# Moving a fifth of the integer shifts of an attention kernel into accumulating DMAs, with output weights loaded late and a fused feature map

## Chip, cores, metric

One core of one Trainium2 chip. The metric is the device time of one execution in microseconds (us), the median of several. Engines: PE is TensorE (matmuls; PEld its weight loads), ACT is ScalarE, DVE is VectorE, POOL is GpSimd, SP is the sync engine, which here only issues DMAs.

## The reference, cut to what matters

```python
x = A_x                                             # 2048 x 512, bfloat16
g = sigmoid((x * gate_w).sum(-1, keepdims=True))
# A: softmax attention, 32 heads of 16 columns
p = softmax(einsum("bhqd,bhkd->bhqk", q, k) * 16**-0.5)
a = einsum("bhqk,bhkd->bhqd", p, v)  # ... @ A_wo
# B: linear attention on the same x
phi = lambda t: where(t > 0, t + 1, exp(t)) + 1e-6
b = (phi(q) @ (phi(k).T @ v)) / (phi(q) @ sum(phi(k)))   # ... @ B_wo
return g * a + (1 - g) * b
```

The exponential of 32 x 2048 x 2048 scores is the bulk of the work: 2048 tiles of 128 x 512.

## The kernel before

The kernel shares these tiles between two engines. ACT takes two at a time with its exponential. DVE takes one at a time with a bit trick: it writes score + constant as a 16-bit integer whose bits are a bfloat16 near the exponential ("op1"). To smooth the trick's error, each such tile is used three times, with 0, 43 and 86 added to the integer, and three value matrices with matched factors. The two extra copies are integer additions, the "shifts". They are made for pairs of tiles, on DVE or on POOL:

```python
def d_finish(cur):                      # both tiles of a pair are converted
    # ... cut ...
    for k, m in enumerate(SHIFTS[1:]):  # SHIFTS = (0, 43, 86)
        dst["shifts"].append((cur, m, z, k + 1))

def cand_shift(E=DV):
    # ... cut: take the next shift, find a free Z slot (16 of them) ...
    if E is PO:
        return C(PO, 400, 70 + 484 * n, lambda: nc.gpsimd.tensor_tensor(
            Z[:, z, 0:512 * n].bitcast(I32), Z[:, z0, 0:512 * n].bitcast(I32),
            mcon[:, kt - 1:kt].to_broadcast([128, 256 * n]), ALU.add), ...)
    # ... cut ...
    return C(DV, 450 if hot else 300, 69 + 134 * n, lambda: nc.vector.tensor_scalar(
        Z[:, z, 0:512 * n], Z[:, z0, 0:512 * n], float(m), None, op0=ALU.add), ...)
```

All instructions are ordered when the kernel is built. A list scheduler carries a clock for each engine, books a duration for each candidate (`70 + 484 * n` ns above), and always places what can start first. The program gives every engine its list, with waits on semaphores in it: in the trace of before POOL is idle for 105.1 us ahead of its shifts, 66.1 us of it ended by DVE's tiles. **So a duration booked too short does not give a wrong result; it puts an instruction in front of others that could have run.** That booked clock is called the schedule here, and no trace shows it. The schedule of the kernel before ends at 672.2 us, 18 us below its time.

The feature map phi of branch B was four operations: exponential on ACT, max on DVE, min on POOL, add on POOL:

```python
yield ac(480, ... activation(eb[:, i, :], bank(b), ACT.Exp) ...)
yield dv(607, ... tensor_scalar(mb[:, i, :], bank(b), 0.0, 1e-6, op0=ALU.max, op1=ALU.add) ...)
yield ("FREE", b)
yield po(640, ... tensor_scalar(eb[:, i, :], eb[:, i, :], 1.0, 0.0, op0=ALU.min, op1=ALU.max) ...)
yield po(1300, ... tensor_tensor(dst_ap, eb[:, i, :], mb[:, i, :], ALU.add) ...)
```

The softmax here doesn't subtract the row's maximum and nothing guards it: scores larger than these inputs give would overflow.

## Time and profile before

| | before |
|---|---|
| time, median | 690.25 us (689.38 to 692.46, four runs) |
| exponentials on ACT (two tiles each) | 707 |
| tiles on DVE | 634 |
| shifts on DVE / POOL | 226 / 408 |

The head of the profile page (busy us of each engine, share of the span, instructions; granted TensorE clock in 40 slices, in tenths):

```profile
span 688.1 us, 24195 instructions
PE 676.8 (98%) x9923; PEld 204.2 (30%) x9923; DVE 607.2 (88%) x1084; ACT 669.2 (97%) x746; POOL 536.8 (78%) x600
...
PEclk9999999999999999999999999999999999999999
```

Groups of instructions of before (line, engine, operation, out<-in, shapes, count | busy us, mean ns of one | idle us before them, and what ended it):

```profile
L750 ACT ACTIVATE P<-ps 128x1024 bf16<-128x1024 f32 x707 | 656.8, 1129 | 5.6 <-PE ps L355 5.6
L723 POOL TENSOR_TENSOR Z<-Z,mcon 128x512 int32<-128x512 int32 x408 | 422.9, 1061 | 105.1 <-DVE Z L671 66.1
L671 DVE TENSOR_SCALAR Z<-ps 128x512 int16<-128x512 f32 x634 | 424.6, 682 | 57.8 <-PE ps L355 52.4
L728 DVE TENSOR_SCALAR Z<-Z 128x1024 int16<-128x1024 int16 x226 | 92.2, 437 | 0.6
...
L1027 POOL TENSOR_TENSOR phiK<-eb,mb 128x512 bf16<-128x512 f32 x32 | 41.0, 1282 | 7.3 <-DVE Z L671 3.0
```

The exponentials (L750) are the limit: ACT is busy all the time and idle before them for only 5.6 us in the whole span. PE shows 98% too, but part of that is filler matmuls on the tile `warm` (703 of them, 76.3 us busy), which the scheduler places in PE's gaps; the granted clock was 1.000 in the mean. To get faster, ACT must get fewer tiles, so DVE must take more.

### The profile page before, as it was taken

The numbers are of one execution on the slowest core, as the hardware profiler recorded it, in microseconds if no ns is written. First come the engines' busy times: TensorE is split into PE (matmuls) and PEld (weight loads), VectorE is DVE, ScalarE is ACT, GpSimd is POOL, SyncE is SP. The second block draws the span as 40 slices with busy tenths as digits, with TensorE's granted clock in tenths as the row PEclk, the third lists the DMA queues.
The fourth block names the chain that finished last, engine by engine and source line by source line (L and its number), as shares of the span: only waits on it lengthen the run. The fifth ranks groups of instructions, "written<-read, shape, count | busy, mean of one in ns | idle before, by whom it ended". The sixth has DMA issues, their size and how long they took to land.

```text
span 688.1 us, 24195 instructions
## 1 busy us (share of the span) xinstructions
PE 676.8 (98%) x9923; PEld 204.2 (30%) x9923; DVE 607.2 (88%) x1084; ACT 669.2 (97%) x746; POOL 536.8 (78%) x600
## 2 busy tenths in 40 slices
PE   8899999999999999999999999999999999999998
PEld 3323232222323232222333323232333322222222
DVE  6799989889988898988889888989889899988995
ACT  6899999999999999999999999999999999999995
POOL 3748888887898879886887888878889985588860
PEclk9999999999999999999999999999999999999999
DMA  6920000000000000000000000000011210000001
GB/s 131 301 66 11 6 5 7 2 10 1 5 8 2 9 4 1 10 2 10 2 11 3 4 9 2 10 2 3 17 25 34 49 25 25 17 10 16 18 17 40
DMA packets 27869, 15.97 MB, mean 23 GB/s; under 512 B 19696, under 2 KB 26736, under 8 KB 27760
## 3 DMA queue, kind: packets, MB, share of 16 engines
q1 hardware_dynamic: 26416, 13.91, 7.6%
q8 instruction: 79, 1.29, 0.8%
q10 hardware_dynamic: 1344, 0.52, 0.3%
q14 instruction: 30, 0.25, 0.1%
HBM read 6.69 MB, written 2.10 MB: 13 GB/s over the span
## 4 chain that ended last, share of the span: by engine, by line
PE 67%; ACT 20%; issue 8%; SPq 2%; DVE 1%; DMA 1%; POOL 0%; ACTq 0%; POOLq 0%
PE ps L355 52%; ACT P L750 19%; PE ps L361 15%; SPq L332 2%; ACT eb L1023 1%; DMA xT<-in_A_x_dram 1%; DVE Z L671 0%; POOL Z L723 0%; DVE Zbd L1057 0%; SPq L336 0%; DVE T L988 0%; ACTq L1407 0%; POOL T L1011 0%; ACT wA L1150 0%; POOLq L1407 0%
## 5 line engine op out<-in xcount | busy, mean ns | idle before, releaser
L750 ACT ACTIVATE P<-ps 128x1024 bf16<-128x1024 f32 x707 | 656.8, 1129 | 5.6 <-PE ps L355 5.6
L723 POOL TENSOR_TENSOR Z<-Z,mcon 128x512 int32<-128x512 int32 x408 | 422.9, 1061 | 105.1 <-DVE Z L671 66.1
L671 DVE TENSOR_SCALAR Z<-ps 128x512 int16<-128x512 f32 x634 | 424.6, 682 | 57.8 <-PE ps L355 52.4
L355 PE MATMUL ps<-Qz,KT 32*128 32x512 bf16 x2048 | 276.3, 384 | 2.5 <-ACT P L750 1.2
L355 PE MATMUL ps<-Z,Vc 128*17 128x512 bf16 x1902 | 269.8, 382 | 1.4 <-DVE T L988 1.1
L355 PE MATMUL ps<-P,Vc 128*17 128x512 bf16 x1414 | 246.2, 383 | 0.0
L355 PEld LDWEIGHTS ps<-Qz,KT 32*128 32x128 bf16 x2048 | 68.8, 91 | 263.8 <-ACT P L750 243.7
L728 DVE TENSOR_SCALAR Z<-Z 128x1024 int16<-128x1024 int16 x226 | 92.2, 437 | 0.6
L355 PEld LDWEIGHTS ps<-Z,Vc 128*17 128x17 bf16 x1902 | 61.4, 88 | 71.4 <-issue 42.5
L355 PE MATMUL ps<-warm 128*32 128x512 bf16 (+18 forms) x703 | 76.3, 335 | 1.4 <-POOL warm L408 1.4
L355 PEld LDWEIGHTS ps<-P,Vc 128*17 128x17 bf16 x1414 | 55.8, 88 | 58.3 <-issue 45.8
L1027 POOL TENSOR_TENSOR phiK<-eb,mb 128x512 bf16<-128x512 f32 x32 | 41.0, 1282 | 7.3 <-DVE Z L671 3.0
L361 PE MATMUL ps<-xT,wA 128*32 128x512 bf16 x512 | 43.5, 383 | 0.9 <-DMA xT<-in_A_x_dram 0.6
L355 PEld LDWEIGHTS ps<-warm 128*32 128x32 bf16 (+1 forms) x703 | 23.0, 95 | 20.7 <-issue 14.1
L988 DVE STREAM_TRANSPOSE T<-ps 128x512 f32<-128x512 f32 x32 | 22.8, 712 | 4.7 <-PE ps L355 4.0
L955 POOL TENSOR_SCALAR Vc<-Vc 128x576 bf16<-128x576 bf16 x32 | 21.9, 684 | 5.7 <-DVE Vc L952 2.0
L1026 POOL TENSOR_SCALAR eb<-eb 128x512 f32<-128x512 f32 x32 | 20.0, 625 | 8.0 <-ACT P L750 2.7
L1024 DVE TENSOR_SCALAR mb<-ps 128x512 f32<-128x512 f32 x32 | 21.8, 680 | 2.5 <-ACT eb L1023 1.9
L1011 POOL TENSOR_TENSOR T<-T,rg 128x256 bf16<-128x256 f32 x31 | 19.5, 628 | 5.1 <-DVE Z L728 1.6
L361 PE MATMUL ps<-wA,xT 128*32 128x128 bf16 x1024 | 21.8, 220 | 1.4 <-issue 1.2
L361 PE MATMUL ps<-xT,wB 128*32 128x512 bf16 x256 | 22.9, 383 | 0.0
L1023 ACT ACTIVATE eb<-ps 128x512 f32<-128x512 f32 x32 | 22.8, 714 | 0.0
(80 smaller groups left out, 303.9 us busy)
## 6 DMA issues: line engine op xcount, KB each, us to landing
Qz<-QT SPq DMA_DIRECT2D x120, 16.0 KB, 1.8
wA<-in_A_wqkv_dram SPq DMA_DIRECT2D x1, 1536.0 KB, 7.1
wB<-in_B_wqkv_dram SPq DMA_DIRECT2D x1, 1536.0 KB, 11.7
xnat<-in_A_x_dram SPq DMA_DIRECT2D x3, 512.0 KB, 12.1
out_dram<-outt SPq DMA_DIRECT2D x12, 128.0 KB, 1.7
woA<-in_A_wo_dram SPq DMA_DIRECT2D x1, 512.0 KB, 13.8
woB<-in_B_wo_dram SPq DMA_DIRECT2D x1, 512.0 KB, 9.5
out_dram<-wA SPq DMA_DIRECT2D x4, 128.0 KB, 1.8
```

What stands on the lines that cost most here:

```text
L355: return lambda: nc.tensor.matmul(o, lhsT=l, rhs=r, start=start, stop=stop, skip_group_check=sg)
L361: h = nc.tensor.matmul(o[32 * j:32 * j + 32], lhsT=l[:, 32 * j:32 * j + 32], rhs=r, start=start, stop=stop, skip_group_check=True)
L671: return C(DV, 400, 533 * n + 74, lambda: nc.vector.tensor_scalar(o, i, ZB, 0.0, op0=ALU.add, op1=ALU.max), [r_bank[b] for b in bks], r_Z[ ...
L723: return C(PO, 400, 70 + 484 * n, lambda: nc.gpsimd.tensor_tensor(Z[:, z, 0:512 * n].bitcast(I32), Z[:, z0, 0:512 * n].bitcast(I32), mcon[ ...
L728: return C(DV, 450 if hot else 300, 69 + 134 * n, lambda: nc.vector.tensor_scalar(Z[:, z, 0:512 * n], Z[:, z0, 0:512 * n], float(m), None, ...
L750: return C(AC, 500, 427 * n + 49, lambda: nc.scalar.activation(P[:, slot, 0:512 * n], bank(b0, n), ACT.Exp, scale=ESC), [r_bank[b0 + k] fo ...
L955: yield po(690, lambda k=k: nc.gpsimd.tensor_scalar(Vc[:, k, vs].rearrange("p a b c -> p (a b c)"), Vc[:, 0, vs].rearrange("p a b c -> p ( ...
L988: yield dv(607, lambda: nc.vector.transpose(T1[:, a, :], bank(7)), [r_bank[7]], [r_T1[a]])
L1023: yield ac(480, lambda: nc.scalar.activation(eb[:, i, :], bank(b), ACT.Exp), [r_bank[b]], [r_eb[i]])
L1024: yield dv(607, lambda: nc.vector.tensor_scalar(mb[:, i, :], bank(b), 0.0, 1e-6, op0=ALU.max, op1=ALU.add), [r_bank[b], r_eb[i]], [r_mb[i]])
L1026: yield po(640, lambda: nc.gpsimd.tensor_scalar(eb[:, i, :], eb[:, i, :], 1.0, 0.0, op0=ALU.min, op1=ALU.max), [r_eb[i]], [r_eb[i]])
L1027: yield po(1300, lambda: nc.gpsimd.tensor_tensor(dst_ap, eb[:, i, :], mb[:, i, :], ALU.add), [r_eb[i], r_mb[i]], dst_res)
```

## The change

The intent: relieve DVE and POOL, so that DVE converts more tiles and ACT fewer. A slot `ZD` is preset by plain DMAs with the constants 43 and 86. Then one DMA with an add, issued on POOL, adds the pair of converted tiles to both halves at once: 512 KB written, in place of two shift instructions. The memory comes from the output weights, which now load late over used parts of `wA`, and from fusing the feature map, which drops a POOL add and a buffer. DVE's shifts also yield when an op1 is about to be ready (`HOLD`).

```diff
+    NZD = 2          # slots
+    ZDD = 1000.0     # booked POOL time of an issue, ns
+    ZDL = 4500.0     # booked time to landing, ns
-        woA = SB([128, NCC, D], BF16, "woA")
-        woB = SB([128, NCC, D], BF16, "woB")
+        woA = wA[:, :, D:2 * D]
+        woB = wA[:, :, 2 * D:3 * D]
+        ZD = SB([128, NZD, NTERM - 1, 512 * NB], I16, "ZD")
+        mrow = SB([128, NTERM - 1, 256], I16, "mrow")
... (the loads of woA and woB move from the start to a task that runs at 23/32 of the rounds)
+        def cand_zfill():                                   # two presets a slot, on SP
...
+                for k in range(NTERM - 1):
+                    fin = dma(SP, ZD[:, i, k, :].rearrange("p (a b) -> p a b", b=256),
+                              mrow[:, k, :].unsqueeze(1).to_broadcast([128, 2 * NB, 256]), semZP[i], ...)
+        def cand_dshift():                                  # one accumulating DMA a pair, on POOL
...
+                fin = dma(PO, ZD[:, i, :, 0:512 * n], Z[:, z, 0:512 * n].unsqueeze(1).to_broadcast([128, NTERM - 1, 512 * n]),
+                          semZA[i], zd_add[i], ZDL, [*r_Z[z][0:n]], [r_ZD[i]], name=f"dshift{i}", issue=ZDD, accum=True)
...
+            if E is DV and dst["op1"]:                      # a shift yields to an op1 that is nearly ready
...
+                if wait < HOLD:
+                    return None
... (phi)
-            yield dv(607, ... mb = max(bank, 0) + 1e-6 ...)
-            yield ("FREE", b)
-            yield po(640, ... eb = min(eb, 1) ...)
-            yield po(1300, ... dst = eb + mb ...)
+            yield po(640, ... eb = min(eb, 1 + 1e-6) ...)
+            yield dv(607, lambda: nc.vector.scalar_tensor_tensor(dst_ap, bank(b), 1e-6, eb[:, i, :], op0=ALU.max, op1=ALU.add), ...)
+            yield ("FREE", b)
```

More of the change, by code (lines that the diff above doesn't have):

```diff
@@ L168, in bass_gated_mix__mha_block__linear_attn_block__prompt_kernel @@
     STICK = 0.0
+    HOLD = 100.0
     NB = 2
@@ L172, in bass_gated_mix__mha_block__linear_attn_block__prompt_kernel @@
     NPS, NZ, NQZ, NVQ = 10, 16, 3, 6
+    NZD = 2
+    ZDD = 1000.0
+    ZDL = 4500.0
+    ZDK = 24
     with ExitStack() as es:
@@ L217, in bass_gated_mix__mha_block__linear_attn_block__prompt_kernel @@
         eb = SB([128, 2, 512], FP32, "eb")
-        mb = SB([128, 2, 512], FP32, "mb")
+        gl = SB([128, 512], FP32, "gl")[:]
+        ZD = SB([128, NZD, NTERM - 1, 512 * NB], I16, "ZD")
+        mrow = SB([128, NTERM - 1, 256], I16, "mrow")
         phiK = SB([128, NKB, D], BF16, "phiK")
@@ L226, in bass_gated_mix__mha_block__linear_attn_block__prompt_kernel @@
         ge = SB([128, NQC, 16], FP32, "ge")
-        gl = mb[:, 0, :]
         gnat = SB([128, NKB], FP32, "gnat")
@@ L245, in bass_gated_mix__mha_block__linear_attn_block__prompt_kernel @@
         r_wA0 = [R(f"wA0{k}") for k in range(3)]
-        r_wA, r_wB, r_woA, r_woB, r_gw = R("wA"), R("wB"), R("woA"), R("woB"), R("gw")
+        r_wA, r_wAk, r_wB, r_gw = R("wA"), R("wAk"), R("wB"), R("gw")
+        r_woA = r_woB = r_wAk
         r_warm, r_ident, r_qmask, r_pidx = R("warm"), R("ident"), R("qmask"), R("pidx")
@@ L261, in bass_gated_mix__mha_block__linear_attn_block__prompt_kernel @@
         r_eb = [R(f"eb{i}") for i in range(2)]
-        r_mb = [R(f"mb{i}") for i in range(2)]
+        r_ZD = [R(f"ZD{i}") for i in range(NZD)]
+        r_mrow = R("mrow")
         r_phiK = [R(f"phiK{i}") for i in range(NKB)]
@@ L322, in bass_gated_mix__mha_block__linear_attn_block__prompt_kernel, with dma @@
         dma_eng = {}
-        def dma(E, o, i, sem, total, lat, reads=(), writes=(), transpose=False, noncontig=False, name="dma", issue=60.0):
+        def dma(E, o, i, sem, total, lat, reads=(), writes=(), transpose=False, noncontig=False, name="dma", issue=60.0, accum=False):
             start = max(E.free, _avail(E, reads, writes))
@@ L330, in go @@
             def go():
+                if accum:
+                    return eng.dma_start(o, i, accum_op=ALU.add)
                 if transpose:
@@ L337, in dma @@
             dd = deps_of(E, reads, writes)
+            if E is PO and gate[0] is not None:
+                dd.append(gate[0])
             E.add(go, dd, inc=False, dma_sem=sem)
@@ L374, in bass_gated_mix__mha_block__linear_attn_block__prompt_kernel @@
         semWA, semWB, semWO, semG = SEM("s_wa"), SEM("s_wb"), SEM("s_wo"), SEM("s_g")
+        semZP = [SEM(f"s_zp{i}") for i in range(NZD)]
+        semZA = [SEM(f"s_za{i}") for i in range(NZD)]
+        zd_fill = [0] * NZD
+        zd_add = [0] * NZD
         semQ = [SEM(f"s_q{i}") for i in range(NQZ)]
@@ L396, in bass_gated_mix__mha_block__linear_attn_block__prompt_kernel @@
         dma(SP, gwc[:], gate_w.rearrange("(cc p) -> p cc", p=128), semG, 16, 3000.0, writes=[r_gw], noncontig=True, issue=500.0)
-        dma(SP, wA[:], wsrc, semWA, 16, 9000.0, writes=[r_wA], issue=500.0)
+        dma(SP, wA[:], wsrc, semWA, 16, 9000.0, writes=[r_wA, r_wAk], issue=500.0)
         dma(SP, wB[:], B_wqkv.rearrange("(cc p) n -> p cc n", p=128), semWB, 16, 12000.0, writes=[r_wB], issue=500.0)
@@ L403, in bass_gated_mix__mha_block__linear_attn_block__prompt_kernel @@
             rr.w = _Raw(semXN, 48)
-        dma(SP, woA[:], A_wo.rearrange("(i p) n -> p i n", p=128), semWO, 32, 16000.0, writes=[r_woA], issue=500.0)
-        dma(SP, woB[:], B_wo.rearrange("(i p) n -> p i n", p=128), semWO, 32, 16000.0, writes=[r_woB], issue=500.0)
-        r_woA.w = _Raw(semWO, 32)
         emit(PO, 300, lambda: nc.gpsimd.memset(warm[:], 0.0), writes=[r_warm])
@@ L425, in bass_gated_mix__mha_block__linear_attn_block__prompt_kernel @@
         for k, m in enumerate(SHIFTS[1:]):
+            emit(PO, 200, lambda k=k, m=m: nc.gpsimd.memset(mrow[:, k, :], m), writes=[r_mrow])
             emit(PO, 150, lambda k=k, m=m: nc.gpsimd.memset(mcon[:, k:k + 1], m * 65537), writes=[r_mcon])
@@ L451, in bass_gated_mix__mha_block__linear_attn_block__prompt_kernel @@
         }
+        port = {"pool": 0.0, "dve": 0.0}
         uq = [[collections.deque(range(NKB)) for _ in range(4)] for _ in range(NR)]
@@ L460, in bass_gated_mix__mha_block__linear_attn_block__prompt_kernel @@
         z_pend = [0] * NZ
+        zd_pend = [0] * NZD
+        zd_ready = [None] * NZD
+        dsh = collections.deque()
         pvi = [[[] for _ in range(4)] for _ in range(NR)]
-        dst = {"cur": None, "open": 0, "op1": collections.deque(), "shifts": collections.deque()}
+        dst = {"cur": None, "opened": [], "op1": collections.deque(), "shifts": collections.deque()}
         owner = {6: None}
@@ L543, in d_batch @@
                 free = [z for z in range(NZ) if not z_pend[z]]
-                if len(free) < NTERM + len(dst["shifts"]) + (NTERM - 1) * dst["open"]:
+                pair = None
+                hr = min(head(j) for j in range(4))
+                if hr < NR and st["s_left"][hr] > ZDK:
+                    pair = [i for i in range(NZD) if zd_ready[i] is not None and not zd_pend[i]]
+                    pair = min(pair, key=lambda i: zd_ready[i]) if pair else None
+                if len(free) < (NTERM if pair is None else 1) + len(dst["shifts"]) + sum(1 if c["pair"] is not None else NTERM - 1 for c in dst["opened"]):
                     return None
@@ L549, in d_batch @@
                 z_pend[z] = 1
-                dst["open"] += 1
-                dst["cur"] = {"todo": NB, "z": z, "units": [], "done": 0}
+                dst["cur"] = {"todo": NB, "z": z, "units": [], "done": 0, "pair": pair}
+                dst["opened"].append(dst["cur"])
+                if pair is not None:
+                    zd_pend[pair] = 1
             return dst["cur"]
@@ L691, in d_finish @@
             z = cur["z"]
-            dst["open"] -= 1
+            dst["opened"].remove(cur)
+            if cur["pair"] is not None:
+                dsh.append(cur)
+                return
             z_pend[z] += NTERM - 2
@@ L695, in d_finish, with go, rel @@
                 dst["shifts"].append((cur, m, z, k + 1))
+        def cand_zfill():
+            for i in range(NZD):
+                if zd_ready[i] is None and not zd_pend[i]:
+                    break
+            else:
+                return None
+            def go():
+                zd_fill[i] += 16 * (NTERM - 1)
+                for k in range(NTERM - 1):
+                    fin = dma(SP, ZD[:, i, k, :].rearrange("p (a b) -> p a b", b=256),
+                              mrow[:, k, :].unsqueeze(1).to_broadcast([128, 2 * NB, 256]), semZP[i], zd_fill[i], 2600.0,
+                              [r_mrow], [r_ZD[i]] if k == 0 else [], name=f"zfill{i}")
+                r_ZD[i].tw = fin
+                zd_ready[i] = fin
+            return C(SP, 400, 120, ("CALL", go), [r_mrow], [r_ZD[i]], lambda fin: None, f"zfill{i}")
+        def cand_dshift():
+            if not dsh:
+                return None
+            cur = dsh[0]
+            i, z, n = cur["pair"], cur["z"], len(cur["units"])
+            def go():
+                dsh.popleft()
+                zd_add[i] += 16
+                fin = dma(PO, ZD[:, i, :, 0:512 * n], Z[:, z, 0:512 * n].unsqueeze(1).to_broadcast([128, NTERM - 1, 512 * n]),
+                          semZA[i], zd_add[i], ZDL, [*r_Z[z][0:n]], [r_ZD[i]], name=f"dshift{i}", issue=ZDD, accum=True)
+                z_pend[z] -= 1
+                zd_pend[i] = n * (NTERM - 1)
+                zd_ready[i] = None
+                def rel():
+                    zd_pend[i] -= 1
+                for k, (r, kb, j) in enumerate(cur["units"]):
+                    for t in range(NTERM - 1):
+                        add_item(r, kb, j, ZD[:, i, t, 512 * k:512 * (k + 1)].bitcast(BF16), r_ZD[i], rel, t + 1, f"d{t + 1}")
+                STATS["shdma"] = STATS.get("shdma", 0) + 1
+            return C(PO, 450, ZDD, ("CALL", go), r_Z[z][0:n], [r_ZD[i]], lambda fin: None, f"dshift{i}")
         def cand_pshift():
@@ L725, in cand_shift @@
                     mcon[:, kt - 1:kt].to_broadcast([128, 256 * n]), ALU.add), [*r_Z[z0][0:n], r_mcon], r_Z[z][0:n], after, f"pshift {m}")
+            if E is DV and dst["op1"]:
+                bk = dst["op1"][0][2][0]
+                wait = max(DV.free, t_free(bk)) - max(DV.free, port["pool"], _avail(DV, r_Z[z0][0:n], r_Z[z][0:n]))
+                if wait < HOLD:
+                    return None
             pr = st["pv_round"]
@@ L867, in wA_cols @@
             base = kind * D + 128 * t8
-            return (lambda cc: wA[:, cc, base:base + 128]), r_wA
+            return (lambda cc: wA[:, cc, base:base + 128]), (r_wAk if kind else r_wA)
         def t_x0():
@@ L968, in t_gate @@
                                            for cc in (2 * h, 2 * h + 1)], [r_xT[qc][h], r_gwr], [r_bank[b]])
-                yield dv(607, lambda b=b: nc.vector.transpose(gl, bank(b)), [r_bank[b]], [r_gl, r_mb[0]])
+                yield dv(607, lambda b=b: nc.vector.transpose(gl, bank(b)), [r_bank[b]], [r_gl])
                 yield ("FREE", b)
                 yield po(250, lambda qc=qc: nc.gpsimd.tensor_copy(ge[:, qc, :], gl.rearrange("p (a b) -> p a b", b=32)[:, :, 0]),
-                         [r_gl, r_mb[0]], [r_ge])
+                         [r_gl], [r_ge])
             phi_free[0] = True
@@ L1023, in phi, with t_wo @@
             yield ac(480, lambda: nc.scalar.activation(eb[:, i, :], bank(b), ACT.Exp), [r_bank[b]], [r_eb[i]])
-            yield dv(607, lambda: nc.vector.tensor_scalar(mb[:, i, :], bank(b), 0.0, 1e-6, op0=ALU.max, op1=ALU.add), [r_bank[b], r_eb[i]], [r_mb[i]])
+            yield po(640, lambda: nc.gpsimd.tensor_scalar(eb[:, i, :], eb[:, i, :], 1.0 + 1e-6, 0.0, op0=ALU.min, op1=ALU.max), [r_eb[i]], [r_eb[i]])
+            yield dv(607, lambda: nc.vector.scalar_tensor_tensor(dst_ap, bank(b), 1e-6, eb[:, i, :], op0=ALU.max, op1=ALU.add),
+                     [r_bank[b], r_eb[i]], dst_res)
             yield ("FREE", b)
-            yield po(640, lambda: nc.gpsimd.tensor_scalar(eb[:, i, :], eb[:, i, :], 1.0, 0.0, op0=ALU.min, op1=ALU.max), [r_eb[i]], [r_eb[i]])
-            yield po(1300, lambda: nc.gpsimd.tensor_tensor(dst_ap, eb[:, i, :], mb[:, i, :], ALU.add), [r_eb[i], r_mb[i]], dst_res)
             phi_free[i] = True
+        def t_wo():
+            yield ("WAIT", lambda: all((NT8 - 1, t) in K_ready and (NT8 - 1, t) in V_ready for t in range(NQC)))
+            yield ("DMA", woA, A_wo.rearrange("(i p) n -> p i n", p=128), semWO, 32, 5000.0, [], [r_wAk], False, True)
+            yield ("DMA", woB, B_wo.rearrange("(i p) n -> p i n", p=128), semWO, 32, 5000.0, [], [r_wAk], False, False)
+            r_wAk.w = _Raw(semWO, 32)
+            yield ("FLAG", lambda: flags.add("wo"))
         def t_phik(tb):
@@ L1121, in t_final @@
             qc, qbl = qb // 4, qb % 4
-            yield ("WAIT", lambda: ("ob", qb) in flags and (tail or ("oat", NT8 - 1, qc) in flags))
+            yield ("WAIT", lambda: "wo" in flags and ("ob", qb) in flags and (tail or ("oat", NT8 - 1, qc) in flags))
             if tail:
@@ L1168, in bass_gated_mix__mha_block__linear_attn_block__prompt_kernel @@
         add_task(t_v(0, 3), -1, 0, "V0,3")
+        add_task(t_wo(), 23, 24, "WO")
         add_task(t_gate(), 0, 1, "GATE")
@@ L1334, in bass_gated_mix__mha_block__linear_attn_block__prompt_kernel @@
         guard = 0
-        port = {"pool": 0.0, "dve": 0.0}
         while True:
@@ L1347, in bass_gated_mix__mha_block__linear_attn_block__prompt_kernel @@
             cands = cand_tasks()
-            for f in (cand_s, cand_dsolo, cand_pv, cand_op1, cand_shift, cand_pshift, cand_exp):
+            for f in (cand_zfill, cand_dshift, cand_s, cand_dsolo, cand_pv, cand_op1, cand_shift, cand_pshift, cand_exp):
                 c = f()
@@ L1389, in bass_gated_mix__mha_block__linear_attn_block__prompt_kernel @@
                 port[c.E.name] = start + c.dur + 20.0
-            if isinstance(c.fns, tuple) and c.fns[0] == "DMA":
+            fin = 0.0
+            if isinstance(c.fns, tuple) and c.fns[0] == "CALL":
+                c.fns[1]()
+            elif isinstance(c.fns, tuple) and c.fns[0] == "DMA":
                 _, o, i, sem, tot, lat, rd, wr, tr, chk = c.fns[1]
```

## The prediction

> **What bounds the kernel now.** The busy table says PE 98%, ACT 97%, DVE 88%, POOL 78%, at a full PE clock. ACT is the limit. In the trace its 707 softmax exponentials start 904 ns apart (the mode; mean 927 for two in a row): 707 x 904 ns is 639 of 688 us, and everything over 904 ns between two of them adds up to only 15 us. PE looks as full, but by starts some 74 us of its time are warm-up filler. So the time falls only if ACT gets fewer score tiles. There are 2048 tiles: 1414 on ACT, 634 on DVE ("op1", 682 ns each, about 600 ns start to start). Every tile moved from ACT to DVE takes 452 ns off ACT.
>
> A DVE tile needs two shifted copies, made by pairs: 226 shifts on DVE (437 ns; 332 ns start to start) and 408 on POOL (1061 ns). DVE is occupied about 82% by starts. A score group on PE holds two ACT tiles plus at most two DVE tiles: 612 of 708 groups carry one, 86 none, 10 two.
>
> **What the change does.**
> 1. About 64 of 317 pairs get both copies from one accumulating DMA (512 KB), so some 130 of 634 shifts leave DVE and POOL: up to 43 us of DVE or 135 us of POOL.
> 2. It adds about 64 DMA issues on POOL. The code books 1 us each, so 64 us of POOL; the trace has none to compare. [...]
> 3. It adds about 130 plain preset DMAs of 256 KB on the sync queue. Estimate: 67 MB in all, about 100 GB/s, where the page shows 23 GB/s, 294 in the loading stage.
> 4. The feature map loses the 1282 ns POOL add, 41 us in all. DVE keeps one pass. The PSUM bank is held about 1.5 to 2 us longer, 32 times.
> 5. Output weights load late: 1 MB out of the start, off the critical path.
> 6. A DMA-shifted pair needs one Z slot instead of three.
>
> **On the critical path:** only the number of ACT tiles. If DVE and POOL keep their present occupancy, the balance closes at about 657 DVE tiles: 23 tiles x 452 ns = 10 us. If each score group carried one DVE tile there would be 683: minus 22 us.
>
> **Predicted:** 677 us (-1.9%), 664 to 690 in 8 of 10. Faster by over 2%: 0.46; within 2%: 0.46; slower: 0.08.
>
> **What would show the steps.** Exponentials fall from 707 to 690-696, op1 rises to 655-670. DVE shifts fall most (226 to about 140), POOL shifts to about 370. An accumulating DMA lands 4 to 5 us after its issue.  The POOL add of 1282 ns is gone.
>
> **What would make it wrong.** The schedule is fixed at build time from a booked landing of 4.5 us. If the DMA lands later [...], PE stops in order at the value products, then ACT: 64 stalls of 1 us would eat all gain. So would a POOL held much longer than 1 us per issue. If phi's longer hold on its bank delays keys or values, ACT runs dry. If instead slots were the limit, not DVE, more groups carry a DVE tile and the gain passes 3%.

## The result and the profile after

The changed kernel takes **764.37 us** (761.70 to 767.77, four runs), before 690.25. The ratio is 1.107 (95% interval 1.102 to 1.113). The output is right.

The head of the page of after:

```profile
span 761.2 us, 24386 instructions
PE 696.5 (91%) x9910; PEld 207.4 (27%) x9910; DVE 604.2 (79%) x1027; ACT 666.5 (88%) x732; POOL 561.0 (74%) x623
...
PEclk9979999999999989999999999999999898989999
```

The groups that answer to those of before:

```profile
L825 ACT ACTIVATE P<-ps 128x1024 bf16<-128x1024 f32 x693 | 652.4, 1062 | 75.6 <-PE ps L367 74.2
L696 DVE TENSOR_SCALAR Z<-ps 128x512 int16<-128x512 f32 x663 | 444.8, 683 | 125.8 <-PE ps L367 120.9
L793 POOL TENSOR_TENSOR Z<-Z,mcon 128x512 int32<-128x512 int32 x398 | 422.9, 1141 | 113.4 <-DVE Z L696 95.5
...
L340 POOL DMA_DIRECT2D ZD<-Z x63 | 76.7, 1233 | 32.8 <-DMA ZD<-mrow 12.4
...
L803 DVE TENSOR_SCALAR Z<-Z 128x1024 int16<-128x1024 int16 (+1 forms) x140 | 65.8, 484 | 0.6
```

The intended shift of work took place: 693 exponentials instead of 707, 663 tiles on DVE instead of 634. But ACT is now idle for 75.6 us before its exponentials instead of 5.6, nearly all of it ended by PE. Every engine is less busy in share: nobody is short of throughput, everybody waits. Why does PE come late? These are lines of the list of waits of after (who waits <- for whom: us in total, times, longest us):

```profile
ACT P L825 <- PE ps L367: 74.2, 71, 8.6
PE ps L367 <- DMA ZD<-Z: 40.2, 35, 3.1
PEld ps L367 <- DMA ZD<-Z: 28.9, 26, 2.9
...
POOL ZD L340 <- DMA ZD<-mrow: 12.4, 1, 12.4
```

PE stands before value products that read a DMA-shifted pair. (The waits of PE and PEld partly cover the same time, so they are not to be added.) The DMA parts of the page say how long these transfers take (first the queue of the accumulating DMAs: packets, MB, share of the 16 DMA engines' span; then issues with KB each and median us to landing):

```profile
q0 software_dynamic: 17136, 33.03, 25.5%
...
ZD<-mrow SPq DMA_DIRECT2D x130, 256.0 KB, 3.1
ZD<-Z POOLq DMA_DIRECT2D x63, 512.0 KB, 6.3
```

Booked were 4.5 us; the median is 6.3. The trace ties only 31 of the 63 landings to their issues: they come 5.0 to 8.5 us after it, never under the booking. (In e1 below, the same DMAs with all 63 landings tied, it is 5.0 to 8.6 us, median 5.9.) Two reasons can be read. Of the 17136 packets, each of the 16 engines handles 17 per DMA (17136 / 63 / 16). Their share of 25.5% of 16 x 761 us is 181 ns for one packet in the mean, so a DMA occupies the DMA engines for 17 x 181 ns = 3.1 us; in the packet records the first one starts 1.8 us after the issue. That makes 4.9 us for a DMA that runs alone (an estimate from these two). And they seldom run alone: both slots come free at about the same time, every 20 us or so, so the DMAs come in couples, mostly 1 to 3 us apart, and the second stands behind the first.

One couple, in the timelines of after (start us, us, engine, line, instruction, count, [idle before <- releaser]). POOL issues two accumulating DMAs at 246.39:

```profile
246.39 2.46 POOL L340 DMA_DIRECT2D ZD<-Z  x2
247.96 4.93 POOL L793 TENSOR_TENSOR Z<-Z,mcon 128x512 int32<-128x512 int32 x4
```

The chain of waits shows the second landing 8.52 us after its issue at 247.21, and PE starting again after it:

```profile
247.12 0.09 issue
247.21 8.52 DMA ZD<-Z
255.73 0.14 issue
255.87 4.33 PE ps L367 x42
```

PE had been idle for 3.11 us, in front of a group of products of which six read `ZD`, and the score products behind it start only after that:

```profile
255.87 0.39 PE L367 MATMUL ps<-P,Vc 128*17 128x512 bf16 x2 [3.11 <-DMA ZD<-Z]
255.87 0.60 PE L367 MATMUL ps<-ZD,Vc 128*17 128x512 bf16 x6
256.41 0.39 PE L367 MATMUL ps<-Qz,KT 32*128 32x512 bf16 x3
```

ACT, which lives from these score products, was idle for 2.67 us, though its next exponential does not need that DMA:

```profile
253.05 1.13 ACT L825 ACTIVATE P<-ps 128x1024 bf16<-128x1024 f32 x1
256.85 1.02 ACT L825 ACTIVATE P<-ps 128x1024 bf16<-128x1024 f32 x1 [2.67 <-PE ps L367]
258.51 1.02 ACT L825 ACTIVATE P<-ps 128x1024 bf16<-128x1024 f32 x1 [0.64 <-PE ps L367]
```

The stalls have a second price. By the clock records of this trace 55 us of the span were granted half the clock, nearly all in stretches of 3.4 us and multiples of it, against 2.9 us before; the mean granted clock is 0.960 to 0.968 in the four runs, and 0.983 to 0.990 in those of e1 below, where PE does not wait for landings. In the 3.41 us before the nine drops between 250 and 715 us PE was busy for 0.8 to 1.9 us. At 257.4, just after the stall above, one such stretch begins, and the next exponential waits another 0.64 us for PE.

To find all of the loss and not only the clearest stalls, I compared the start of each exponential in the trace with its start in the schedule. Before, they drift apart by 13.7 us over the whole span; after, by 92.7 us. The drift after grows in about 30 jumps of 1 to 3 us, about one for each couple of DMAs, and one of 9 us at the start, where the first accumulating DMA held POOL for 12.4 us behind a preset that stood in the sync queue after the weight loads (the last of the waits above).

### The profile page after: what moved, and what is told of

Its sections match the earlier page's. It is cut to its first block, busy times and chain, and to the rows that moved or that the text cites. A ratio compares the mean times of both kernels' runs of the same rounds, so it can differ in the third digit from the quotient of the medians.

```text
span 761.2 us, 24386 instructions
## 1 busy us (share of the span) xinstructions
PE 696.5 (91%) x9910; PEld 207.4 (27%) x9910; DVE 604.2 (79%) x1027; ACT 666.5 (88%) x732; POOL 561.0 (74%) x623
## 3 DMA queue, kind: packets, MB, share of 16 engines
q0 software_dynamic: 17136, 33.03, 25.5%
## 4 chain that ended last, share of the span: by engine, by line
PE 49%; DMA 27%; POOL 10%; DVE 7%; issue 4%; SPq 3%; ACT 0%; POOLq 0%; DVEq 0%
PE ps L367 38%; DMA ZD<-Z 24%; PE ps L373 11%; POOL Z L793 4%; DVE Z L696 4%; POOL ZD L340 2%; SPq L342 2%; DMA xnat<-wA 2%; DMA ZD<-mrow 1%; DVE T L1063 1%; POOL T L1086 1%; POOL Vc L1030 1%; SPq L346 1%; POOL eb L1099 1%; DMA xT<-in_A_x_dram 1%
## 5 line engine op out<-in xcount | busy, mean ns | idle before, releaser
L825 ACT ACTIVATE P<-ps 128x1024 bf16<-128x1024 f32 x693 | 652.4, 1062 | 75.6 <-PE ps L367 74.2
L696 DVE TENSOR_SCALAR Z<-ps 128x512 int16<-128x512 f32 x663 | 444.8, 683 | 125.8 <-PE ps L367 120.9
L367 PE MATMUL ps<-P,Vc 128*17 128x512 bf16 x1385 | 258.4, 393 | 27.8 <-DMA ZD<-Z 17.8
L340 POOL DMA_DIRECT2D ZD<-Z x63 | 76.7, 1233 | 32.8 <-DMA ZD<-mrow 12.4
L367 PE MATMUL ps<-warm 128*32 128x512 bf16 (+13 forms) x632 | 74.1, 328 | 1.4 <-POOL warm L421 1.4
L367 PE MATMUL ps<-ZD,Vc 128*17 128x512 bf16 x252 | 60.0, 407 | 12.2 <-DMA ZD<-Z 12.2
L803 DVE TENSOR_SCALAR Z<-Z 128x1024 int16<-128x1024 int16 (+1 forms) x140 | 65.8, 484 | 0.6
L373 PE MATMUL ps<-wA,xnat 128*32 128x512 bf16 x256 | 23.5, 392 | 0.0
L373 PE MATMUL ps<-wA,OAT 128*32 128x512 bf16 x256 | 23.1, 381 | 0.0
L373 PE MATMUL ps<-wB,xT 128*32 128x512 bf16 x256 | 22.8, 382 | 0.0
L373 PE MATMUL ps<-phiK,xnat 128*32 128x512 bf16 x256 | 21.7, 385 | 0.0
```

Source lines behind the costliest of these rows:

```text
L340: return eng.dma_start(o, i, accum_op=ALU.add)
L367: return lambda: nc.tensor.matmul(o, lhsT=l, rhs=r, start=start, stop=stop, skip_group_check=sg)
L373: h = nc.tensor.matmul(o[32 * j:32 * j + 32], lhsT=l[:, 32 * j:32 * j + 32], rhs=r, start=start, stop=stop, skip_group_check=True)
L696: return C(DV, 400, 533 * n + 74, lambda: nc.vector.tensor_scalar(o, i, ZB, 0.0, op0=ALU.add, op1=ALU.max), [r_bank[b] for b in bks], r_Z[ ...
L825: return C(AC, 500, 427 * n + 49, lambda: nc.scalar.activation(P[:, slot, 0:512 * n], bank(b0, n), ACT.Exp, scale=ESC), [r_bank[b0 + k] fo ...
```

## The experiments

Theory A: the landing waits on PE, with the clock drops they cause, are the loss. Rival B: the DMA path costs by its mere presence: POOL's issue time, the presets in the sync queue, the traffic; or the other parts of the change (fused feature map, late weights, yielding shifts) do.

| run | what | schedule, us | time, us | ratio to before |
|---|---|---|---|---|
| after | the change | 666.5 | 764.37 | 1.107 |
| e1_no_landing_wait | products read a ready tile | 666.5 | 711.87 | 1.029 |
| e2_book_8us | landing booked at 8 us | 667.4 | 718.39 | 1.040 |
| e3_no_dma | no DMA path | 667.8 | 692.29 | 1.002 |
| e5_one_slot | one slot | 665.7 | 716.08 | 1.037 |
| e4_late_first | no DMA path before 50 us | 663.2 | 756.54 | 1.095 |
| e7_zero_late | e4 with a ready tile | 663.2 | 714.57 | 1.035 |
| e6_book_queue | e4 with queue-aware booking | 666.9 | 711.09 | 1.029 |
| e8_presets_unread | e3 plus presets | 667.8 | 697.23 | 1.011 |
| e9_adds_unread | e8 plus adds | 677.6 | 719.84 | 1.041 |
| e10_more_slots | no DMA path, 20 Z slots | 666.1 | 686.68 | 0.994 |
| e11_no_hold | no DMA path, no yielding | 667.6 | 687.80 | 0.996 |
| e12_tuned_dma | DMA path, bookings mended | 669.8 | 699.00 | 1.012 |

Two kernels give a wrong result (e1 and e7, relative errors 0.099 and 0.091); all others are right.

### e1: the same instructions without the wait

```diff
-   add_item(r, kb, j, ZD[:, i, t, 512 * k:512 * (k + 1)].bitcast(BF16), r_ZD[i], rel, t + 1, f"d{t + 1}")
+   add_item(r, kb, j, warm[:], r_fk[i], rel, t + 1, f"d{t + 1}")   # r_fk: ready from the start, but booked like ZD
```

The order of all instructions on all engines was checked to be that of after; only PE's operand and its waits differ.

> The changed kernel with every instruction, its order, and all DMAs and presets kept; only the 252 value products of the DMA-shifted pairs read a tile of zeros that is ready from the start, so TensorE never waits for an accumulating DMA (wrong result on purpose). Theory A (TensorE stops in order for landings later than the booked 4.5 us, and the stops also drop its clock): falls from 764 to about 690-700, exponentials back to under 30 us over 904 ns apart, apart from the stall of about 9 us near the start. Rival B (the issues on POOL, the preset traffic, the DMA bandwidth or the other parts of the change cost the time): stays above 735.

Measured: 711.87 us. So 52.5 us of the 74 us are landing waits and their clock drops, with every DMA, preset and issue still there. Theory A has the larger part; the expected 690 to 700 was too low, so B has a part as well. ACT's idle time before its exponentials, in the waits of e1:

```profile
ACT P L825 <- PE ps L367: 27.6, 25, 7.4
```

### e2: book the landing honestly

```diff
-    ZDL = 4500.0
+    ZDL = 8000.0
```

> Only the booked landing of an accumulating DMA changed, 4.5 to 8 us, so the schedule places its value products later; still 63 such DMAs. Theory A: measured landings are 5.0 to 8.5 us, so nearly all waits for ZD go; 690-705 us, mean TensorE clock above 0.985. Rival B: still about 760, since work and DMAs are the same.

Measured: 718.39 us, clock 0.979. The right result, 63 DMAs as before, and 46 us less from one booked number. Of the waits for landings this is what is left (waits of e2):

```profile
PEld ps L367 <- DMA ZD<-Z: 1.3, 1, 1.3
PE ps L367 <- DMA ZD<-Z: 1.0, 1, 1.0
```

The waits went as A expects, but the time is 13 us over the range, and the clock is under the 0.985 that I expected. 26 us remain over e3 (below), in e1 20 us, that are not waits for landings.

### e3: the change without its DMA path

```diff
-                if zd_ready[i] is None and not zd_pend[i]:    # in cand_zfill
+                if False:
```

> The rest of the change alone: no presets, no accumulating DMAs, all shifts on DVE and POOL; fused feature map, late output weights, shifts that yield to a ready eviction stay. 701 exponentials against 707 of before. Theory A: no loss is left, 680-688 us (before: 690). If the longer hold of the feature map's bank or the late weights are part of the loss: 695 or more.

Measured: 692.29 us, ratio 1.0017 (0.9985 to 1.0048). That is over the expected 680 to 688 us, so the gain that I expected of the rest of the change is missing, but under the 695 us of a loss: the rest of the change carries none of the 74 us that is clear of noise. The run also shows how little there was to win: its schedule ends at 667.8 us, and that of the full change at 666.5. By the scheduler's own booking, the DMA path was worth 1.4 us (667.84 less 666.48).

### e5: one slot

```diff
-    NZD = 2
+    NZD = 1
```

> One preset slot instead of two, booked landing still 4.5 us: 34 accumulating DMAs, and none can queue behind another. Theory A, with the refinement that the second DMA of a couple waits for the first: each now lands about 5.1 us after its start, so each wait is about 0.6 us instead of 2: 700-715 us. If the loss goes simply by the number of DMAs (34 of 63): about 728.

Measured: 716.08 us, a little over the range and well below the 728 of a loss by count. The 34 DMAs land 5.04 us after their issue at the least, median 5.4 us, against 5.9 in e1 with two slots. This supports the refinement: the second of a couple queues behind the first. Alone, a DMA is still over the booking every time, by up to 2.7 us (7.2 us), so that queue is not the only delay; the others were not looked into.

### e4 and e7: the stall at the start

```diff
-   if hr < NR and st["s_left"][hr] > ZDK:
+   if hr < NR and st["s_left"][hr] > ZDK and PE.free > 50000.0:
```

e7 has in addition the edit of e1.

> The changed kernel, but no pair uses the DMA path before 50 us of the schedule; booked landing still 4.5 us, 61 accumulating DMAs. The first accumulating DMA stood 12.4 us on POOL behind a preset that queued after the weight loads. If that start stall is worth what the drift between schedule and trace shows (about 9 us, of which the schedule itself gives 3 more): 750-757 us. If the landing waits are all there is: 760 or more.

Measured: 756.54 us (749.20 to 760.19), within the range. That is 8 us less than the change, of which its shorter schedule gives 3.

> The schedule of the run above (late first use), with the value products of DMA-shifted pairs reading a ready tile of zeros (wrong result on purpose): no start stall and no landing waits. If the two together are nearly the whole loss: 695-702 us. What is above the 692 us of the kernel without DMAs, less the fewer exponentials, is other cost of the DMA path.

Measured: 714.57 us: a miss. Without start stall and landing waits it should have fallen to 702 or less, and it is not even below e1. What the start gave back was lost elsewhere, and the trace of e7 shows two places. The first: DVE's timeline around 376 us.

```profile
375.41 0.69 DVE L696 TENSOR_SCALAR Z<-ps 128x512 int16<-128x512 f32 x1 [0.17 <-PE ps L367]
376.02 5.07 DVE L803 TENSOR_SCALAR Z<-Z 128x1024 int16<-128x1024 int16 x1
381.01 1.28 DVE L696 TENSOR_SCALAR Z<-ps 128x512 int16<-128x512 f32 x2
```

A shift that takes 0.42 us took 5.07 us. POOL's timeline of the same stretch:

```profile
373.56 1.21 POOL L340 DMA_DIRECT2D ZD<-Z  x1 [1.04 <-DVE Z L696]
374.34 6.46 POOL L793 TENSOR_TENSOR Z<-Z,mcon 128x512 int32<-128x512 int32 x6
```

POOL ran six shifts in a row, right behind an issue, and DVE's shift got through when they were over: the row ended at 380.80, the shift at 381.09. (Their records overlap: each lasts 1.5 us, and the next starts 1.0 us after it, so POOL was never free in between.) So here the wait covered a whole row of POOL instructions whose records overlap. Where they overlapped by 0.04 us only, in e11 at 353.67 us, a DVE shift got in after the first POOL shift and took 1.03 us. The scheduler is written to place DVE's shifts and POOL's work apart; but it does so by its booked times, and here, behind an issue that took 1.21 us where 1 us was booked, the two met. The second place: the output stage, where DVE waits for the DMA transposes of branch B, 12.0 us in all in e7 (3.9 us in e1, 1.7 us in e3). That these two make up the whole difference is not shown.

### e6: a booking that knows the queue

```diff
+   fin = max(fin, zq[0] + ZQL)       # not before the DMA in front has landed, plus 3.4 us
+   zq[0] = r_ZD[i].tw = fin
-    ZDL = 4500.0
+    ZDL = 5600.0
```

and the late first use of e4.

> Right result: late first use, and a booking that knows the queue: 5.6 us from issue, and at least 3.4 us after the one before has landed. 60 accumulating DMAs. If booking was the fault: at most a few waits for ZD stay, 695-705 us, below the 718 of the flat 8 us booking. If 712 or more, another cost of the DMAs counts.

Measured: 711.09 us (ratio 1.024 to 1.035, so about 707 to 714): right result, 7 us better than the flat 8 us (though with the late first use besides), but above the range. Waits for landings are gone here too (1.5 us of PEld in all). Another 19 us over e3 belong to something else.

### e8: presets that nobody needs

e3 with the presets sent at the cadence of the changed kernel and never read (112 of them); the compute engines' lists are those of e3.

```diff
-                if False:
+                if PE.free > zd_next[i] and PE.free < 630000.0 and not zd_due[i]:   # every 21.3 us
```

> The kernel without the DMA path (692 us), same schedule to the instruction on the four compute engines, plus 112 preset DMAs of 256 KB at the cadence of the changed kernel, which nobody reads and no accumulating DMA follows. If the presets cost nothing: 692 within 0.5%. If they hold up the sync queue (0.65 us of issue each, and the transposes and query scatters stand in line behind them): 695-699 us.

Measured: 697.23 us, within the second range, 4.9 us over e3, which ran on another chip (ratios 1.0106 and 1.0017 to before, intervals apart only just: 1.0078 to 1.0135 and 0.9985 to 1.0048). DVE's wait for the transposes rises from 1.7 us to this (waits of e8), while the median transpose lands 2.5 us after its issue in both runs, which fits with its being issued later and not carried slower:

```profile
DVE wA L1195 <- DMA xnat<-wA: 5.7, 3, 4.1
```

The sync queue's timeline shows how presets and transposes share it; this is from e1, in the output stage:

```profile
556.66 1.36 SPq L342 DMA_TRANSPOSE xnat<-wA  x1
558.16 1.37 SPq L346 DMA_DIRECT2D ZD<-mrow  x2
559.62 1.31 SPq L342 DMA_TRANSPOSE xnat<-wA  x1
561.02 1.29 SPq L346 DMA_DIRECT2D ZD<-mrow  x2
562.40 6.46 SPq L342 DMA_TRANSPOSE xnat<-wA  x3
```

Two presets hold the queue for 1.3 us, as long as a transpose; the scheduler books 0.06 us each.

### e9: adds that nobody needs

e8 plus 56 accumulating DMAs on POOL (source: a constant weight tile), whose sums nobody reads.

```diff
+   dma(PO, ZD[:, i, :, :], wB[:, 0, 0:1024].bitcast(I16).unsqueeze(1).to_broadcast([128, NTERM - 1, 1024]), ..., issue=ZDD, accum=True)
```

> As the run with unread presets, plus 56 accumulating DMAs on POOL (booked 1 us each) into the slots, which nobody reads; all shifts stay on DVE and POOL. The schedule itself is 9.8 us longer (710 exponentials, since POOL loses 56 us and takes no shift less). If an add costs POOL no more than is booked: 697 + 10 = 707 us. [...]: 712 or more, POOL shifts mean above 1100 ns (1054 without adds).

Measured: 719.84 us. Booking accounts for 9.8 us of the step from 697.23; 12.8 us come on top. POOL's own group in e8:

```profile
L795 POOL TENSOR_TENSOR Z<-Z,mcon 128x512 int32<-128x512 int32 x489 | 502.4, 1054 | 61.8 <-DVE Z L698 44.8 <-DVE Z L805 7.5 <-PE ps L367 5.6
```

and in e9, with the issues:

```profile
L807 POOL TENSOR_TENSOR Z<-Z,mcon 128x512 int32<-128x512 int32 x437 | 471.7, 1152 | 56.7 <-DVE Z L698 23.1 <-DVE Z L817 22.4 <-PE ps L367 7.0
...
L340 POOL DMA_DIRECT2D ZD<-wB x56 | 73.6, 1354 | 12.3 <-DVE Z L817 10.5 <-PE ps L367 1.4 <-issue 0.2
```

A POOL shift is now recorded at 1152 ns in the mean, at most 2194 where 1272 was the most in e8, without adds. These longer records are not POOL time to be added up, for they overlap. In a row behind one issue each shift is recorded at about 1.5 us, behind two at about 1.9, but the next starts 1.0 us after it as before (median 997 ns). In the couple shown above, four such shifts took 4.93 us together. The issue itself lets the next POOL instruction start after 0.8 us, and the row ends about 0.45 us late, once. So an issue costs POOL about 1.2 us, as long as its own record, where 1 us was booked (an estimate from these records). DVE's shifts rise from 432 to 488 ns in the mean, eight of them over 1 us. What share of the 12.8 us each of these has is not shown; DVE's wait for the transposes rose too, from 5.7 to 10.1 us.

### e10, e11: what the change is worth without DMAs

e11 is e3 with `HOLD = -1e9` (no yielding). e10 is e11 with `NZ = 20`: the memory of the DMA slots given to four more ordinary Z slots.

> No DMA path; the memory of the preset slots goes to 4 more ordinary Z slots (20), and DVE shifts do not yield. Right result. 698 exponentials, the schedule is 6.1 us shorter than before. If schedules without DMAs keep the offset of before (18 us from schedule to time): 684-687, within 1% of before. If the offset is that of the kernel without DMAs (24 us): 690.

> No DMA path, 16 slots, DVE shifts do not yield: that is fused feature map and late weights alone. 701 exponentials, schedule 4.5 us shorter than before. If the fused feature map and the late weights cost nothing on the chip: 685-688. If one of them costs: 690-693, as with the yielding.

Measured: 686.68 us (ratio 0.994, 0.992 to 0.997) and 687.80 us (0.996, 0.993 to 0.998). Both beat before by about half a per cent, clear of noise and well within 2%. So the fused feature map and the late weights cost nothing and give 0.4% (e11); the longer hold of the bank that I feared is not seen. e3 with its yielding shifts is 4.5 us slower than e11 on a schedule of the same length; they ran on different chips, each beside runs of before, and why was not looked into.

### e12: the DMA path with everything known put in

```diff
-    ZDD = 1000.0
-    ZDL = 4500.0
+    ZDD = 1600.0
+    ZDL = 6000.0     # and 3.6 us behind the one before
+   ... and 50000.0 < PE.free < 510000.0:     # first and last use
```

> The DMA path with every booking mended: landing 6 us and 3.6 us behind the one before, 1.6 us of POOL per issue, first use after 50 us, last use at 510 us of the schedule so that no preset stands before the output transposes; 47 accumulating DMAs. Schedule 669.8 us. If those were all of its hidden costs: 688-694. If DMAs still cost more than they save: 696 or more; it would then lose to the kernel without DMAs (692).

Measured: 699.00 us with 47 accumulating DMAs. Mended bookings, with 47 DMAs in place of 63, take back 65 us of 74. But it is still slower than before (1.012, 1.009 to 1.014; within 2%), and 7 us slower than e3, which does without. The 1.6 us booked for an issue are more than the 1.2 us read in e9, so the run does not show what exact bookings would give.

## Why the prediction was wrong, point by point

**Right: what bounds the kernel, and how far the work would move.** I expected 690 to 696 exponentials and 655 to 670 tiles on DVE; there are 693 and 663. DVE shifts fell to 140 as I said; POOL's to 398, where I had said about 370. The POOL add of the feature map is gone. That 14 fewer exponentials mean 14 x 904 ns = 12.7 us less on ACT held for the schedule too: its last exponential ends 11.7 us earlier.

**Wrong, and the step that failed: "An accumulating DMA lands 4 to 5 us after its issue", with nothing in the sum for its wait.** I took the landing from the number booked in the code, named a later landing as a risk ("PE stops in order at the value products, then ACT: 64 stalls of 1 us would eat all gain"), and gave slower only 0.08. The mechanism was named; its size was set to zero. Measured: 5.0 us at the very least, median 6.3 of the 31 that the trace ties (5.9 of all 63 in e1), up to 8.5. Taking the wait away alone (e1) gives 52.5 us back, that is 0.83 us for each of 63 DMAs, clock drops included. A hint was there: the booking had no record in the trace behind it. Nor did I ask what two of them in a row would do. And the packet records of the change do not show that a DVE shift at the same time makes such a DMA start late: of the 33 DMAs with no other still moving 1 us after their issue, 13 had such a shift between issue and first packet and 20 had none, and in both groups the first packet starts 1.8 us after the issue (median).

**Wrong in size: POOL's issue.** I used the booked 1 us. In e9 an issue costs POOL about 1.2 us, and in e7 a DVE shift waited through a row of POOL shifts behind an issue (5.07 us); the 56 adds cost 12.8 us above the booked part, which is not divided between these.

**Wrong: presets as bandwidth alone.** I counted them in GB/s and had nothing for them on the critical path. The mean rate came out as I estimated (109 GB/s). But the sync queue is a line, and each preset stands in it for about 0.65 us, in front of transposes: 4.9 us (e8).

**Wrong: the gain itself.** I equated 23 tiles with 10 us. The schedule ends only 5.7 us earlier, though its last exponential ends 11.7 us earlier: 192 products of the final projection come after the last exponential where 92 did before, and this tail grew from 8.4 to 14.2 us in the trace. And 4.3 of those 5.7 us belong to the rest of the change, as e3's schedule shows.

**The sum.** From before to after, 74 us: 52.5 by landing waits (e1), 19.6 between e1 and e3, and 2.0 between e3 and before. The 19.6 us agree roughly with presets and adds measured alone (4.9 and 12.8 us), though these were measured on another schedule, and the start stall has its share in them. Not settled: how the 52.5 us divide into standing still and running at half clock, and the exact share of the start stall, since taking it away saved 8 us in e4, 3 of them by a shorter schedule, and nothing in e7.

## What to carry to other kernels

In a kernel whose order is fixed when it is built, a booked latency is a promise by the slowest case: an engine that stops in order for one late operand starves those that live from its next instruction (here PE stood for 3.11 us, and ACT behind it for 2.67 us). Measure a new kind of operation by itself, in the rhythm in which it will be used (here two at a time), before booking it, and book late rather than early. And ask first what the scheduler itself says the idea is worth: here 1.4 us, for a path that cost some 20 us even when nobody waited for it.

## The hardware figures of this case

- An accumulating DMA from SBUF to SBUF: each DMA engine took 191 ns per packet of 2 KB (3.1 us for 512 KB, about 170 GB/s); the landing was 5.0 us alone at the least and up to 8.5 us behind another (packets and the last figure from the change, 5.0 from e5).
- Its issue on POOL: the record lasts 1.2 us in the mean in the change (1233 ns; 1354 in e9), in e9 the next POOL instruction starts 0.8 us after it, and shifts behind issues are recorded at up to 2.2 us instead of 1.04, overlapping, with starts still 1.0 us apart.
- DVE's shifts beside POOL's: one DVE shift waited through a row of overlapping POOL shifts, 5.07 us (e7).
- A plain preset of 256 KB held the sync queue for about 0.65 us of the 3.1 us to its landing (e1, and the page of the change), and 112 of them cost 4.9 us (e8).
- PE's clock: in the trace of the change all drops lie on one grid of 3.41 us; each follows a grid window in which PE was busy for 1.91 us or less, and none follows a window of 1.94 us or more (one window of 1.83 us, near the end, was not followed by a drop).
